# One lasting PSUM piece for the cell, scores ahead of updates, and another order on VectorE

## The chip, the cores and the metric

The kernel runs on one core of one Trainium2 chip. The metric is the device time of one execution in microseconds, given as the median of several runs. TensorE is called PE in the profile, VectorE DVE, ScalarE ACT, GpSimd POOL, and SyncE, which issues nearly all of the transfers, SP.

## The reference

An mLSTM cell over 4 batches, 8 heads, 768 time steps and head size 40, followed by a multiplicative feed-forward layer over the 3072 tokens with 320 features:

```python
for t in range(S):
    m_new = np.maximum(f_gate[:, :, t] + m, i_gate[:, :, t])
    f_stab = np.exp(f_gate[:, :, t] + m - m_new)
    i_stab = np.exp(i_gate[:, :, t] - m_new)
    C = f_stab[:, :, None, None] * C + i_stab[:, :, None, None] * np.einsum('bhd,bhe->bhde', vt, kt)
    n = f_stab[:, :, None] * n + i_stab[:, :, None] * kt
    h_tilde = np.einsum('bhde,bhe->bhd', C, qt)
    denom = np.maximum(np.abs(np.einsum('bhd,bhd->bh', n, qt)[:, :, None]), 1.0)
    y[:, :, t] = 1.0 / (1.0 + np.exp(-o_gate[:, :, t])) * h_tilde / denom
# x: y as (3072 tokens, 320)
out = ((x @ w1) * (x @ w2) @ w3) @ w_out      # d_ff = 1024
```

The four weights come as 64-bit floats and are turned into 32-bit floats on the chip.

## The kernel before, in words

**Chunks and units.** Time is cut into chunks of 64 steps. Two chunks (128 steps) of one batch, with all 8 heads, are a unit n; there are 24 units, and n runs over the 4 batches first. Inside a chunk the recurrence is a masked product: scores of k and q, times weights, times v; what the chunk inherits is the state times q.

**One step of the loop.** The main loop (L595) has 30 steps s. In a step it issues the loads two units ahead (`load`, `load_o`; `load_u` three ahead), the decay of the first state of the unit on POOL (`decayed`, L305), the turns of k and q (`turn`, L283: for n < 10 TensorE transposes `pt` and ScalarE copies, later a VectorE transpose), turns of y (`x_trans`, tile `px`), products of the feed-forward layer (`up`: tiles `pa` and `pb`; `ffn_out`: tile `po`; `w3_mm`: tile `wp`), and then the cell in `quarter_work` (L310). The ups are cut so that a small remainder (`rest`, 64-row matmuls) runs at the start of `quarter_work`; each up ends in a ScalarE copy `a_sb` and a VectorE product `ab`. From s = 4 on there is one up in a step, from s = 6 on there are two. Behind the cell VectorE converts pieces of the weights (`convert`), two or three in most steps up to s = 15.

**The cell.** `quarter_work(s)` issues the outputs of unit s-1 and the updates and scores of unit s, as small matmuls of 64 columns in quarters of the array. Its results lie in a tile `cell` of four PSUM banks, the only one of its pool (`bufs=1`):

```python
ss, pc, pi = part(0, 0, L), part(0, NP * L, D1), part(2, 0, D1)
ph = [t[halves[x], 2 + x, NP * D1:(NP + H) * D1].rearrange("p (h d) -> p h d", d=D1) for x in range(2)]
```

Banks 0 and 1 hold the scores `ss` and the updates `pc` of unit s; banks 2 and 3 hold what unit s-1 inherits (`pi`) and its own part (`ph`). The tile is taken anew in every step, so its first matmul waits until all readers of the tile of the step before are done. Within a step, accesses of different engines to the same bank wait for each other, and accesses to different banks do not.

**Order on TensorE before:** `ph`, `pi`, `pc`, `ss`. **Order on VectorE before:** the weights times scores (L348, tile `pw`), the second state (L352 or L354), the outputs (L369 and twice L373, tile `h`), the denominators (three small instructions from L378 on, tile `den`), the output gate (L383, tile `o_in`), y (L385), and last the third state (L362). The third state is the second one decayed by POOL (L307) plus the second half of `pc`.

**What sets the order.** TensorE's instructions are chained in the order written (`in_order`). For the first 17 steps all other engines keep the written order too (`keep_order`, `pinned = 17`), SP's and POOL's transfers among them; later a planner places instructions, except where `issue_after` ties them behind another one: the work behind the first read of `ss`, and the turns and conversions behind what `quarter_work` returns. Four more PSUM banks (`ps_m`) go round among all other matmul results while the cell runs.

## Time and profile before

| What | us |
|---|---|
| median of 11 runs | 472.02 |
| fastest and slowest of them | 469.83 and 474.42 |
| the profiled execution | 470.55 |
| its span on the core | 468.5 |
| TensorE busy in it | 446.8 |
| VectorE busy | 258.0 |
| ScalarE busy | 134.1 |
| POOL busy | 82.0 |

The span is what the profile covers of the execution; the rest of its time lies around it. A row of the profile gives line, engine, operation and tiles, as output<-inputs; nearly all matmuls carry line 90 or 93, those of the helpers, so they are told apart by their tiles. "PEld" is the load of weights into the array, which overlaps the matmuls. The busy time of TensorE holds pipelined instructions whose ends are modelled, so it tells that TensorE had work, not how well it was used. The row PEclk is the clock that TensorE was granted, in tenths of full speed, in 40 slices of 11.7 us.

### The profile page before, as it was taken

The numbers are of one execution on the slowest core, as the hardware profiler recorded it, in microseconds if no ns is written. First come the engines' busy times: TensorE is split into PE (matmuls) and PEld (weight loads), VectorE is DVE, ScalarE is ACT, GpSimd is POOL, SyncE is SP. The second block draws the span as 40 slices with busy tenths as digits, with TensorE's granted clock in tenths as the row PEclk, the third lists the DMA queues.
The fourth block names the chain that finished last, engine by engine and source line by source line (L and its number), as shares of the span: only waits on it lengthen the run. The fifth ranks groups of instructions, "written<-read, shape, count | busy, mean of one in ns | idle before, by whom it ended". The sixth has DMA issues, their size and how long they took to land.

```text
span 468.5 us, 12799 instructions
## 1 busy us (share of the span) xinstructions
PE 446.8 (95%) x5319; PEld 359.4 (77%) x5319; DVE 258.0 (55%) x515; ACT 134.1 (29%) x376; POOL 82.0 (17%) x156
## 2 busy tenths in 40 slices
PE   2867999999999999999999999999999999999997
PEld 2766788888778788887878777787777877868864
DVE  6675589888988988988832451615426133011110
ACT  3653274434533244223451220311101101011111
POOL 5341222222220221122161111200000000000000
PEclk9986699999999999999999999999999999999999
DMA  9999957688987676687462635444121120200001
GB/s 186 170 175 204 192 89 156 152 182 168 213 197 182 143 161 161 160 162 143 96 119 63 127 87 125 95 106 109 32 63 31 34 63 2 62 15 14 1 14 44
DMA packets 136554, 52.72 MB, mean 113 GB/s; under 512 B 109936, under 2 KB 127536, under 8 KB 136496
## 3 DMA queue, kind: packets, MB, share of 16 engines
q1 hardware_dynamic: 132896, 47.87, 49.8%
q10 hardware_dynamic: 3600, 4.03, 2.5%
q8 instruction: 42, 0.69, 0.7%
q14 instruction: 16, 0.13, 0.1%
HBM read 46.07 MB, written 5.80 MB: 111 GB/s over the span
## 4 chain that ended last, share of the span: by engine, by line
PE 93%; issue 2%; ACT 1%; DVE 1%; DMA 1%; POOL 1%; SPq 0%; DVEq 0%; POOLq 0%; ACTq 0%
PE pa L90 27%; PE po L90 22%; PE pb L90 18%; PE cell L90 13%; PE wp L90 7%; PE pt L93 2%; PE px L93 1%; DMA kbuf<-in_k_dram 1%; PE ub L90 1%; ACT pw L278 1%; POOL vw L302 0%; POOL pw L280 0%; SPq L444 0%; ACT qT L297 0%; PE pg L93 0%
## 5 line engine op out<-in xcount | busy, mean ns | idle before, releaser
L569 DVE TENSOR_TENSOR ab<-pb,a_sb 128x512 f32<-128x512 f32 x48 | 32.7, 689 | 140.7 <-ACT a_sb L568 140.7
L90 PE MATMUL po<-w3o,ab 128*128 128x320 f32 x384 | 106.2, 435 | 0.0
L90 PEld LDWEIGHTS po<-w3o,ab 128*128 128x128 f32 x384 | 72.1, 190 | 30.1 <-ACT a_sb L568 0.4
L90 PE MATMUL pa<-xT,w 128*128 128x256 f32 x384 | 92.8, 385 | 0.6 <-ACT xT L423 0.6
L90 PE MATMUL pb<-xT,w 128*128 128x256 f32 x384 | 91.7, 382 | 0.0
L90 PEld LDWEIGHTS pa<-xT,w 128*128 128x128 f32 x384 | 73.4, 193 | 13.5 <-ACT xT L423 1.0
L90 PEld LDWEIGHTS pb<-xT,w 128*128 128x128 f32 x384 | 73.8, 192 | 10.3
L568 ACT ACTIVATE a_sb<-pa 128x512 f32<-128x512 f32 x48 | 28.7, 597 | 170.2 <-PE pb L90 170.2
L307 POOL TENSOR_TENSOR state<-state,decay 128x164 f32<-128x164 f32 x40 | 21.9, 549 | 202.6 <-DVE state L352 113.6
L90 PE MATMUL pa<-xT,wr 64*64 64x256 f32 x384 | 47.0, 383 | 0.0
L90 PE MATMUL pb<-xT,wr 64*64 64x256 f32 x384 | 47.0, 383 | 0.0
L278 ACT ACTIVATE pw<-pw,aT 128x64 f32<-128x64 f32 x160 | 40.3, 337 | 14.8 <-DMA pw<-U_d 14.8
L90 PEld LDWEIGHTS pa<-xT,wr 64*64 64x64 f32 x384 | 25.8, 132 | 16.8 <-issue 7.8
L90 PE MATMUL wp<-wo,w3T 128*128 128x320 f32 x128 | 35.9, 433 | 0.6 <-DVE ab L569 0.6
L280 POOL TENSOR_SCALAR_AFFINE_SELECT pw<-pw 64x512 f32<-64x512 f32 x48 | 32.9, 686 | 19.0 <-ACT pw L278 17.5
L90 PEld LDWEIGHTS cell<-vbuf,pw 64*64 64x64 f32 x768 | 28.2, 144 | 9.3 <-issue 6.4
L90 PE MATMUL cell<-vbuf,pw 64*64 64x41 f32 x768 | 28.2, 234 | 5.6 <-issue 5.6
L348 DVE TENSOR_TENSOR pw<-cell,pw 128x512 f32<-128x512 f32 x24 | 16.6, 690 | 30.3 <-PE cell L90 30.3
L576 ACT COPY o_sb<-po 128x320 f32<-128x320 f32 x24 | 10.1, 420 | 75.5 <-PE po L90 71.6
L90 PEld LDWEIGHTS wp<-wo,w3T 128*128 128x128 f32 x128 | 23.7, 190 | 9.7 <-DVE ab L569 0.9
L90 PEld LDWEIGHTS pb<-xT,wr 64*64 64x64 f32 x384 | 25.8, 132 | 0.0
L373 DVE TENSOR_TENSOR h<-cell,h 64x328 f32<-64x328 f32 x48 | 23.9, 497 | 1.1
(90 smaller groups left out, 456.8 us busy)
## 6 DMA issues: line engine op xcount, KB each, us to landing
raw<-in_moe_w_dram SPq DMA_DIRECT2D x64, 128.0 KB, 3.1
pw<-U_d SPq DMA_DIRECT2D x40, 128.0 KB, 3.9
kbuf<-in_k_dram SPq DMA_DIRECT2D x24, 160.0 KB, 4.6
vbuf<-in_v_dram SPq DMA_DIRECT2D x24, 160.0 KB, 4.8
o_in<-in_o_gate_dram SPq DMA_DIRECT2D x24, 160.0 KB, 4.6
out_dram<-o_sb ACTq DMA_DIRECT2D x24, 160.0 KB, 2.0
raw<-in_moe_w_dram SPq DMA_DIRECT2D x7, 512.0 KB, 5.7
raw<-in_moe_w_out_dram SPq DMA_DIRECT2D x32, 80.0 KB, 2.4
```

The costliest lines, as they stand in the source:

```text
L90: in_order(nc.tensor.matmul(out, lhsT=lhsT, rhs=rhs, start=start, stop=stop))
L93: in_order(nc.tensor.transpose(out, in_, ident[0:n, 0:n]))
L278: nc.scalar.activation(out=pw[:, h, :], in_=src[:, h, :], func=AF.Exp, bias=aT[:, c, b * H + h:b * H + h + 1])
L280: nc.gpsimd.affine_select(out=pw[r], in_=pw[r], compare_op=OP.is_ge, fill=0.0, base=0, pattern=[[0, H], [1, L]], channel_multiplier=-1)
L307: nc.gpsimd.tensor_tensor(out=new, in0=old, op=OP.mult, in1=decay[:, b * NP:(b + 1) * NP, 2 * c + x:2 * c + x + 1] .to_broadcast([P, NP, D1]))
L348: first_read = nc.vector.tensor_tensor(out=pv, in0=ss, in1=pv, op=OP.mult)
L373: nc.vector.tensor_tensor(out=h[r], in0=ph[x], in1=h[r], op=OP.add)
L568: nc.scalar.mul(out=a_sb, in_=pa, mul=UP ** -2)
L569: nc.vector.tensor_tensor(out=ab_t[gr][j][:, fs[0]:fs[-1] + 1, t0:t0 + a_sb.shape[-1]], in0=pb, in1=a_sb, op=OP.mult)
L576: nc.scalar.copy(out=o_sb, in_=po)
```

## The change

Three things are changed in the cell, and nothing in the loads, the feed-forward layer or the order of the steps.

- The four banks are taken once, ahead of the loop, and serve all steps. There is no hand-over of the tile between steps any more; accesses to the same banks still wait for each other.
- On TensorE the scores `ss` are issued ahead of the updates `pc`.
- On VectorE the outputs (`h`) come first, then the weights (`pw`), the second state, the denominators, the third state, and last the output gate and y. For this `outputs` is cut into three: the part that reads PSUM, `first` (denominators) and `then` (gate and y). What `quarter_work` returns, behind which the turns and conversions are tied, is y in every step that has one.

```diff
@@ -72,6 +72,8 @@
     ps_c = cell_psum.enter_context(tc.tile_pool(name="ps_c", bufs=1, space=bass.MemoryType.PSUM))
     banks = [ps_m]
 
+    cell = ps_c.tile([P, 4, 512], FP, name="cell", tag="cell")
+
     def mps(shape, name):
         pool = banks.pop(0)
         banks.append(pool)
@@ -311,7 +313,7 @@
 
 
         rest()
-        t = ps_c.tile([P, 4, 512], FP, name="cell", tag="cell")
+        t = cell
 
         def part(j, c0, n):
             return t[:, j:j + 2, c0:c0 + NP * n].rearrange("p x (n d) -> p x n d", d=n)
@@ -336,17 +338,22 @@
             first, second, after = state[b]
             before_t[n] = first, second
             state[b] = after, second, first
+            kT, qT, pw = kT_t.pop(n), qT_t[n], u_t[n]
+            for p in range(NP):
+                for hip, x in quarters:
+                    mm(ss[halves[x], hip, p, :], kT[heads[hip], p, halves[x]], qT[heads[hip], p, halves[x]])
             for p in range(NP):
                 for x, e in quarters:
                     if x in ends:
                         mm(pc[halves[e], x, p, :], kt[halves[x], 2 * p + e, :], vw[halves[x], 2 * p + e, :])
-            kT, qT, pw = kT_t.pop(n), qT_t[n], u_t[n]
-            for p in range(NP):
-                for hip, x in quarters:
-                    mm(ss[halves[x], hip, p, :], kT[heads[hip], p, halves[x]], qT[heads[hip], p, halves[x]])
+        den = None
+        if 0 <= s - 1 < NU:
+            den = outputs(s - 1, pi, ph)
+        if n < NU:
             pv = pw.rearrange("p (n two) t -> p two n t", two=2)
             first_read = nc.vector.tensor_tensor(out=pv, in0=ss, in1=pv, op=OP.mult)
-            with tc.issue_after(first_read.ins):
+        with tc.issue_after(first_read.ins) if first_read else nullcontext():
+            if n < NU:
 
                 if c:
                     nc.vector.tensor_tensor(out=second, in0=pc[:, 0], in1=second, op=OP.add)
@@ -354,13 +361,13 @@
                     nc.vector.tensor_copy(out=second, in_=pc[:, 0])
                 if len(ends) > 1:
                     decayed(after, second, n, 1)
-        done = None
-        with tc.issue_after(first_read.ins) if first_read else nullcontext():
-            if 0 <= s - 1 < NU:
-                done = outputs(s - 1, pi, ph)
+            if den:
+                done = den()
             if n < NU and len(ends) > 1:
-                done = nc.vector.tensor_tensor(out=after, in0=pc[:, 1], in1=after, op=OP.add)
-        return done
+                nc.vector.tensor_tensor(out=after, in0=pc[:, 1], in1=after, op=OP.add)
+            if den:
+                done = done()
+        return done if den else first_read
 
     def outputs(n, pi, ph):
         c, b = divmod(n, B)
@@ -375,15 +382,23 @@
 
 
         den = sb.tile([P, H, 1], FP, name="den", tag="den")
-        nc.vector.tensor_scalar(out=den.bitcast(U32), in0=h[:, :, D:D1].bitcast(U32), scalar1=0x7FFFFFFF, scalar2=None,
-                                op0=OP.bitwise_and)
-        nc.vector.tensor_scalar(out=den, in0=den, scalar1=1.0, scalar2=2.0, op0=OP.max, op1=OP.mult)
-        nc.vector.reciprocal(out=den, in_=den)
-        e = o_t.pop(n)
-        nc.vector.scalar_tensor_tensor(out=e, in0=e, scalar=1.0, in1=den.to_broadcast([P, H, D]), op0=OP.add, op1=OP.mult)
-        y_t[n] = sb.tile([P, DM + REM], FP, name="y", tag="y")
-        return nc.vector.tensor_tensor(out=y_t[n][:, 0:DM].rearrange("p (h d) -> p h d", d=D), in0=h[:, :, 0:D], in1=e,
-                                op=OP.mult)
+
+        def first():
+            V = nc.vector
+            V.tensor_scalar(out=den.bitcast(U32), in0=h[:, :, D:D1].bitcast(U32), scalar1=0x7FFFFFFF, scalar2=None,
+                            op0=OP.bitwise_and)
+            V.tensor_scalar(out=den, in0=den, scalar1=1.0, scalar2=2.0, op0=OP.max, op1=OP.mult)
+            V.reciprocal(out=den, in_=den)
+            return then
+
+        def then():
+            e = o_t.pop(n)
+            nc.vector.scalar_tensor_tensor(out=e, in0=e, scalar=1.0, in1=den.to_broadcast([P, H, D]), op0=OP.add, op1=OP.mult)
+            y_t[n] = sb.tile([P, DM + REM], FP, name="y", tag="y")
+            return nc.vector.tensor_tensor(out=y_t[n][:, 0:DM].rearrange("p (h d) -> p h d", d=D), in0=h[:, :, 0:D],
+                                           in1=e, op=OP.mult)
+
+        return first
 
     def send(n):
 
```

## The prediction

> **What bounds the kernel now.** I read the page first (busy rows, clock row, chain), then the chain in order of time, the timeline where the chain shows gaps, and the transfers.

> ```profile
> span 468.5 us, 12799 instructions
> PE 446.8 (95%) x5319; PEld 359.4 (77%) x5319; DVE 258.0 (55%) x515; ACT 134.1 (29%) x376; POOL 82.0 (17%) x156
> ...
> PEclk9986699999999999999999999999999999999999
> DMA  9999957688987676687462635444121120200001
> ```

> TensorE is 95% busy and at full clock except between about 32 and 56 us (slices of 11.7 us), and the DMA engines are full (9) in the first five slices, to 58.6 us. The time is therefore the TensorE work plus what the start loses. The chain in order of time shows the loss:

> ```profile
> 29.55 3.13 issue
> 32.68 4.61 PE cell L90 x128
> 37.29 1.80 PE pt L93 x8
> 39.43 2.46 issue
> 41.90 3.82 PE cell L90 x105
> ...
> 165.79 2.32 PE cell L90 x123
> ```

> Columns are start, length, what. pt are the turns of k and q, px that of y, pa and pb the ups. The same cell block takes 4.61 us at 32.68 and 2.32 at 165.79. Two gaps of 3.13 and 2.46 us stand in front of cell blocks, put down to "issue", that is, to nothing the profile can name. From 70 us to the last matmul the chain has no gap over 0.7 us. The timeline names the gaps' end:

> ```profile
> 32.25 0.33 DVE L362 TENSOR_TENSOR state<-cell,state 128x164 f32<-128x164 f32 x1
> ...
> 32.65 1.71 PEld L90 LDWEIGHTS cell<-vbuf,pw 64*64 64x64 f32 x30 [3.36 <-issue]
> ...
> 41.47 0.33 DVE L362 TENSOR_TENSOR state<-cell,state 128x164 f32<-128x164 f32 x1
> ...
> 41.87 1.46 PEld L90 LDWEIGHTS cell<-vbuf,pw 64*64 64x64 f32 x31 [2.69 <-issue]
> ```

> Both times TensorE starts 0.07 us after the last VectorE read of the previous cell tile (32.58 to 32.65, 41.80 to 41.87). So the wait is the handing back of the whole four-bank tile, whose last reader is the third state update behind the y chain. In later steps the ups (6.9 us) and the remainders stand in between, and this wait is covered.

> **The change, part by part.** I number steps by s; ph, pi are the outputs' two matmul groups, pc the updates, ss the scores.

> *One lasting piece.* The release is gone; what stays are the waits between accesses of the same banks. ph and pi (banks 2, 3) now wait only for the three h reads and for the weights of the step before; ss and pc (banks 0, 1) for the third state read. At s=2: updates of step 1 end at 27.4 before. With scores first they end about 27.0 (copies of kT, qT end 25.58; 0.7 each for ss and pc). ub takes 1.1, so 28.1; the turns need q of step 2, issued at 24.02, landing 4.6 later, 28.6; they end about 29.2. ph and pi follow at once (1.5, at 30.7) instead of at 32.65. ss needs qT, whose copy ends at 32.03: ScalarE does the tanh of o_in first, and o_in lands at 26.66 + 3.9 = 30.56 whatever TensorE does. ss and pc run 32.1 to 33.3 (VectorE's third state read of step 1 is long done, POOL's vw ended 32.81 and can be 0.4 earlier). So cell 2 ends at 33.3 and not at 37.29: minus 4.0.

> *What is late next: the loads.* SP issues without a break from 19.9 to 59.2 us, the DMA engines are full, so the loads keep their times.

> ```profile
> 30.06 0.53 SPq L126 DMA_DIRECT2D q_all<-in_q_dram  x1
> ...
> 37.17 0.54 SPq L126 DMA_DIRECT2D kbuf<-in_k_dram  x1
> ```

> These are q for s=3 and k for s=4; the transfers' view gives 5.5 us to landing for the one (35.6) and 5.0 for the other (42.2). Turns of s=3 start about 34.9 with k (estimate, q's 5.5 used) and end between 36.2 (full clock) and 37.1 (half). px and the cell follow without the 2.46 gap: end at 39.0 at full clock (px 0.5, cell 2.3), 42.5 at half (0.8, 4.6); before 47.26. Either way s=4 waits for k until 42.2, so here the clock matters little. Turns end at 43.9 to 44.4 (q about 43.3); pa began 1.2 us behind the turns' end before (49.16 to 50.36, the copies of qT and xT on ScalarE), so 45.1 to 45.6 against 50.36: minus 4.8 to 5.3. From pa to the end of cell 4 it took 10.1 us, mostly at half clock; at full clock it is 3.46 + 0.5 + 0.9 + 2.4 = 7.3. So cell 4 ends at 52.4 to 55.7 against 60.5: minus 4.8 to 8.1.

> [...] In windows of 1 us (the clock is the third column from the end, behind the engines' busy times) the clock falls to 0.5 at about 32.04, rises at 38.87, falls at 42.28, rises at 55.92: the distances are 2, 1 and 4 times 3.41 us.

> ```profile
> 31.00:32.00 1.00, 0.00 (x0) 0.00 (x0) 0.96 (x2) 1.00 (x3) 0.85 (x3) 1.00 1.08 257
> 32.00:33.00 1.00, 0.32 (x7) 0.35 (x8) 0.97 (x3) 0.46 (x2) 1.00 (x2) 0.52 1.46 163
> ```

> [...] By the trace a gap of 2.46 us (39.43 to 41.90) lost the clock, and gaps of about 0.6 us (45.72, 49.79) kept it from coming back. The change still leaves a gap of up to 1.6 us at 33.3 and one of up to 3.2 at 39.0. [...]

> *Outputs first on VectorE.* The h reads can start when pi ends, 1.1 us before the cell's end, beside ss and pc. In a late step: the two ab end at 167.2, h three times (0.49 + 1.01) to 168.7, weights 0.69, state 0.32, denominators 0.8, third state 0.33, e and y 1.3: y at 172.2, against 172.9 before. Weights and second state come about 0.5 us later, so POOL's decay starts later, and behind it the masks (1.37), vw and the next decay: the next cell reads them some 10 us later. y being 0.7 earlier takes away TensorE's wait of 0.45 at 65.41 (px behind y): minus 0.4. The release of o_in for SP's next load hangs on y and comes earlier too. No DMA issue is moved.

> *A new wait.* The third state update now follows the second by only the denominators; it needs POOL's decay (0.47 plus two handoffs of about 0.1). The denominators take 0.8 to 0.9: covered. Bounds: nothing (a wait cannot gain), or 0.3 us on VectorE per step when POOL is still in the previous decay (0.70). e, y, the transposes and conversions, then the next ab queue behind it. Beyond 120 us VectorE has slack; between 61 and 120 (89 to 94% busy in the later slices) five steps make at most 1.5 us, against 1 us a step that VectorE gains by not waiting for the cell's end. I take zero.

> *Order of ss and pc on TensorE.* Same 128 matmuls. No row shows the price of ss after pi; bounds from the cell's own spread in the chain, 2.25 to 2.37 us: from minus 0.1 to plus 0.1 a step, about 2 us over 24 steps either way. I take zero.

> *Sum.* Minus 5.2 (4.8 + 0.4) to minus 8.5 (8.1 + 0.4). The loads cap it: k and q of s=6 land at 59.9 and about 60.5, where the turns began at 69.29, and behind the scaling of the next w_out piece (issued from 59.34) the copies of s=6 wait on ScalarE. I take minus 6.5. From there on everything hangs on TensorE's or VectorE's own pace and shifts as a whole; the weight loads of SP wait for VectorE's conversions and shift with them. The profiled execution took 470.55 (span 468.5 plus 2.05), so 464.05; it lies 1.5 under the median of the runs, which gives 465.5 for the median.

> **The rivals.** *The gain is half given back* (the freed time turns into waits for loads and a half clock that lasts to 56 us, or VectorE's conversions between 60 and 80 us hold ab): minus 2 to 4, 468 to 470. For it: the DMA share is above 1 in 19 of the 30 windows of 1 us from 30 to 60. Against: SP waits 4 us for VectorE at 59 to 69 us, so the loads there would move up. *Nothing changes*, because the gaps are something else (instruction fetch beside the full DMA engines; 0.63 at 45.72 has no releaser) or the dependence still spans the whole piece: minus 0.5, 471.5. Against: twice the same 0.07 us. *Slower: the cell itself stretches*, because VectorE now reads banks 2 and 3 while TensorE writes 0 and 1, in every one of 24 steps. It decides from 0.27 us a cell (6.5 / 24); at 0.5 (ss and pc, 1.1 us, half as fast again) the sum is plus 12 minus 6.5, 477.5. Against: ph took 1.02 us with no VectorE read beside it (57.99) and 1.02 with an ab read of PSUM beside it (165.61).

> **How the numbers follow.** Main case 0.68 (463.5 to 467), half given back 0.16, no change 0.07, slower 0.09. A measurement here can tell about 0.3% (1.4 us). So faster 0.84, same 0.07, slower 0.09. The range goes from 462.5 (8.5 and one more for the order) to 470 (end of the second case).

> **What would show it.** Right: no gap in front of ph at s=2 and s=3; the wait at s=3 and s=4 named after kbuf or q_all; pa of s=4 at 45 to 46; the cell still 2.3 us beyond 70; px at s=5 without wait; the cell of s=23 some 6 us earlier. Wrong: pa still at 50; a cell above 2.5 us in late steps; VectorE's third state waiting on POOL for more than 0.3 us a step; ab late, with TensorE waiting for a bank between 60 and 120.

## The result, and the profile after

The changed kernel takes 465.78 us (median; 463.12 to 468.85 in 12 runs) beside 472.01 us before (465.66 to 474.55, 47 runs): a ratio of 0.991, 95% interval 0.9881 to 0.9939. The forecast was 465.5. The total is right; several steps that led to it are not. A few executions of before and of three experiments took over 1.5% more than the fastest of their kernel; medians and ranges in the text are of all executions, the ratios leave these out.

The page after, first the span, the busy times, TensorE's granted clock and the share of the DMA engines (40 slices, now 11.5 us each):

```profile
span 461.4 us, 12788 instructions
PE 440.7 (96%) x5319; PEld 353.1 (77%) x5319; DVE 262.6 (57%) x515; ACT 134.9 (29%) x376; POOL 82.5 (18%) x156
...
PEclk9997999999999999999999999999999999999999
DMA  9999999797978567676353543535021120200001
```

The same 5319 matmul records take 6.1 us less of TensorE's time (446.8 before), out of 7.1 us of span. Granted clock in windows of a fraction of a microsecond: half speed from 32.0 to 38.9 and 42.3 to 55.9 us before (20.5 us), from 35.9 to 42.7 after (6.8 us). So between these two traces most of the gain is work that is now done at full clock. The trace after is of the shortest of its 12 executions (463.12 us), and traces of other kernels divide a gain of the same size differently, as the experiments show.

The chain in order of time (start, length, what), the stretch that the prediction was about:

```profile
29.61 2.49 PE cell L92 x115
32.10 1.26 issue
33.36 0.37 PE cell L92 x8
...
37.31 4.55 PE cell L92 x124
...
44.65 1.99 PE pa L92 x8
...
49.73 2.35 PE cell L92 x115
```

Cell blocks of s=2 and s=3 begin 3.1 and 4.6 us earlier (32.68 and 41.90 before); `pa` of s=4 begins at 44.65 and not 50.36; the cell of s=4 ends at 52.08 and not 60.54. From there on the kernel is only shifted: the block that took 2.32 us at 165.79 now ends 6.9 us earlier (161.23 against 168.11). A new gap of 1.26 us without a releaser stands inside the cell of s=2.

The timeline of TensorE after, the waits in front of the two cells and in front of `px` at s=5:

```profile
29.61 1.07 PE L92 MATMUL cell<-vbuf,pw 64*64 64x41 f32 x30 [1.06 <-DVE state L367]
...
37.31 1.83 PE L92 MATMUL cell<-vbuf,pw 64*64 64x41 f32 x30 [1.19 <-DVE state L367]
...
57.09 0.41 PE L95 MATMUL px<-ident,y 128*128 128x128 f32 x2 [0.34 <-DVE y L398]
58.58 0.33 PE L95 MATMUL px<-ident,y 128*128 128x128 f32 x1 [1.07 <-POOL y L428]
```

The first product of `ph` writes banks 2 and 3, and still waits for the third state (L367), which reads bank 1. And for the first of the `h` reads, which needs only banks 2 and 3, the view of its line says what it waited for (us in all, times), and VectorE's timeline when it began at s=4:

```profile
L376 DVE TENSOR_TENSOR h<-cell,gT x24: 483/500/501, 26.1 to 387.7; 128x328 f32<-128x328 f32 x24
...
  PE cell L92: 19.8, 20
...
52.11 0.50 DVE L376 TENSOR_TENSOR h<-cell,gT 128x328 f32<-128x328 f32 x1 [1.01 <-PE cell L92]
```

It starts when the cell ends (52.11 against 52.08), not when `pi` ends 1.0 us before. So one lasting piece of four banks is still one thing to the waits between engines; that accesses to different banks of it do not wait for each other, as the description of the kernel before has it, does not hold. Why, then, did the time fall where the prediction said, with the dependence that it had declared gone?

What changed is where the same wait stands. In the traces before and after no matmul and no weight load carries more than one wait (in each of the two, 263 of the 5319 weight loads carry one; a product's wait stands there); what else is waited for stands in a wait instruction of its own ahead of it (68 on TensorE in each, with two waits in 18 of them before and in 12 after). In front of the cell of s=2:

```
            wait instruction                        first product of ph
before      transfer of vbuf, DVE third state       TensorE itself (from the release of the old piece)
after       transfer of vbuf                        DVE third state
```

In the trace before, that wait instruction is recorded from 28.82 to 32.62 us, and the one in front of the cell of s=3 from 36.99 to 41.84; after, the wait instructions there take 0.05 us. The page names the same thing in its way: 5.6 us of idle in front of `ph` "<-issue" before, 2.2 us "<-DVE state L367" after. The next section asks which of these counts.

### The profile page after: what moved, and what is told of

The parts are those of the page before. It is cut to its first block, busy times and chain, and to the rows that moved or that the text cites. A ratio compares the mean times of both kernels' runs of the same rounds, so it can differ in the third digit from the quotient of the medians.

```text
span 461.4 us, 12788 instructions
## 1 busy us (share of the span) xinstructions
PE 440.7 (96%) x5319; PEld 353.1 (77%) x5319; DVE 262.6 (57%) x515; ACT 134.9 (29%) x376; POOL 82.5 (18%) x156
## 4 chain that ended last, share of the span: by engine, by line
PE 91%; DVE 4%; issue 1%; DMA 1%; ACT 1%; POOL 1%; SPq 0%; DVEq 0%; POOLq 0%; ACTq 0%
PE pa L92 27%; PE po L92 23%; PE pb L92 18%; PE cell L92 12%; PE wp L92 8%; PE pt L95 1%; PE px L95 1%; DMA kbuf<-in_k_dram 1%; DVE pw L354 1%; DVE h L380 1%; DVE h L376 0%; PE ub L92 0%; DVE ma L191 0%; ACT kT L299 0%; POOL pw L282 0%
## 5 line engine op out<-in xcount | busy, mean ns | idle before, releaser
L92 PE MATMUL pa<-xT,w 128*128 128x256 f32 x384 | 91.0, 380 | 0.8 <-ACT xT L438 0.8
L92 PEld LDWEIGHTS pa<-xT,w 128*128 128x128 f32 x384 | 72.3, 190 | 13.2 <-ACT xT L438 1.0
L309 POOL TENSOR_TENSOR state<-state,decay 128x164 f32<-128x164 f32 x40 | 19.2, 481 | 207.0 <-DVE den L388 155.3
L92 PE MATMUL wp<-wo,w3T 128*128 128x320 f32 x128 | 35.9, 433 | 1.1 <-DVE ab L584 1.1
L282 POOL TENSOR_SCALAR_AFFINE_SELECT pw<-pw 64x512 f32<-64x512 f32 x48 | 34.3, 715 | 13.1 <-ACT pw L280 11.5
L92 PEld LDWEIGHTS cell<-vbuf,pw 64*64 64x64 f32 x768 | 26.8, 138 | 6.0 <-DVE state L367 2.8
L92 PE MATMUL cell<-vbuf,pw 64*64 64x41 f32 x768 | 26.8, 228 | 2.2 <-DVE state L367 2.2
L304 POOL TENSOR_TENSOR vw<-vbuf,wT 128x328 f32<-128x328 f32 x24 | 19.6, 818 | 22.3 <-PE cell L92 20.8
```

The source lines that it names most:

```text
L92: in_order(nc.tensor.matmul(out, lhsT=lhsT, rhs=rhs, start=start, stop=stop))
L282: nc.gpsimd.affine_select(out=pw[r], in_=pw[r], compare_op=OP.is_ge, fill=0.0, base=0, pattern=[[0, H], [1, L]], channel_multiplier=-1)
L304: nc.gpsimd.tensor_tensor(out=vw_t[n], in0=vbuf[n % NB], op=OP.mult, in1=wT[:, c, b * H:(b + 1) * H].unsqueeze(2).to_broadcast([P, H, D1]))
L309: nc.gpsimd.tensor_tensor(out=new, in0=old, op=OP.mult, in1=decay[:, b * NP:(b + 1) * NP, 2 * c + x:2 * c + x + 1] .to_broadcast([P, NP, D1]))
```

## The experiments

Each of the three parts alone, and a kernel in which the waits really are bank by bank, beside before at 470.82 us (466.23 to 475.85, 23 runs).

**The lasting piece alone** (e1_lasting_only), before with

```diff
+    cell = ps_c.tile([P, 4, 512], FP, name="cell", tag="cell")
-        t = ps_c.tile([P, 4, 512], FP, name="cell", tag="cell")
+        t = cell
```

> Before, with the four banks taken once and nothing else changed. The piece theory (the gain is the missing hand-over: ph waits only for readers of its own two banks): the gaps ahead of the cells of s=2 and s=3 go, and most of the 6 us are here, 466 to 468. The order theory (the whole piece is still waited for, and the gain comes from what stands last among its readers): ph of s=2 and s=3 still starts 0.07 us behind the third state, gaps of about 3.1 and 2.5 us stay, time within 1 us of before.

Measured: 466.30 us (465.31 to 467.82, 6 runs), ratio 0.9904 [0.9876, 0.9933]. The lasting piece alone brings a gain as large as the whole change's. Its timeline:

```profile
32.65 1.82 PE L92 MATMUL cell<-vbuf,pw 64*64 64x41 f32 x30 [3.10 <-DVE state L364]
...
41.75 1.07 PE L92 MATMUL cell<-vbuf,pw 64*64 64x41 f32 x30 [2.17 <-DVE state L364]
...
48.02 1.99 PE L92 MATMUL pa<-xT,w 128*128 128x256 f32 x8 [0.84 <-ACT xT L425]
```

The two cells start at nearly the same times as before (32.68, 41.90), after nearly the same waits (3.15 and 2.48): the wait of which the prediction expected everything is still there in full. But the cell of s=3 has no gap inside (0.63 us at 45.72 before), the clock comes back at 46.15 instead of 55.92, and `pa` starts 2.3 us earlier.

**Scores ahead of updates alone** (e2_scores_only) and **VectorE's new order alone**, with a fresh piece and the updates first (e3_order_only):

```diff
 # e2: before, with the block of ss moved ahead of the block of pc
-            [pc] [ss]
+            [ss] [pc]
 # e3: after, with
-        t = cell
+        t = ps_c.tile([P, 4, 512], FP, name="cell", tag="cell")
 #     and the block of pc ahead of ss again
```

> Before, with the scores issued ahead of the updates and nothing else. Piece theory: minus 0.5 at most. Order theory: the cell of s=0 ends about 1.0 us earlier (the scores no longer wait behind vw), the cell of s=1 about 1.4 us earlier (26.0 against 27.4); the gap ahead of the cell of s=2 stays at about 3 us; in all minus 1 to minus 2.

> Before, with VectorE's new order alone (outputs, weights, second state, denominators, third state, gate, y), the piece taken anew in each step and updates first. Piece theory: no gain beyond 0.5 us. Order theory: the third state ends 1.4 to 1.6 us earlier behind the cell's end, the gaps shrink from 3.1 and 2.5 to about 1.5 and 1 us, minus 3 to minus 5.

Measured: 470.85 us, ratio 0.9988 [0.995, 1.0026], and 470.40 us, ratio 0.9989 [0.9955, 1.0023]. Neither differs from before by anything that can be told. Both traces have gaps inside a cell without a releaser: 2.36 and 2.85 us in the scores-only kernel (at 35.70 and 47.06), 1.51 us in the other.

**Two lasting pieces of two banks** (e4_two_pieces), the changed kernel with

```diff
-    cell = ps_c.tile([P, 4, 512], FP, name="cell", tag="cell")
+    cell = [ps_c.tile([P, 2, 512], FP, name=f"cell{i}", tag=f"cell{i}") for i in range(2)]
-            return t[:, j:j + 2, c0:c0 + NP * n]...
+            return cell[j // 2][:, :, c0:c0 + NP * n]...
```

and `ph` in the second one.

> The changed kernel, with the four banks as two lasting pieces of two banks (scores and updates; inherited part and own part). Piece theory: the same as the changed kernel, since bank by bank is what it already waits for. Order theory: now h starts when pi ends, about 1.0 us ahead of the cell's end, and ph of s=2 and s=3 waits for the weights and h and not for the third state: gaps under 0.5 us at s=2, the loads are the next wait; minus 0 to minus 3 us against the changed kernel, 463 to 466.

Measured: 464.65 us (463.84 to 465.40, 6 runs), ratio 0.9866 [0.984, 0.9892]. Here the waits are what the prediction had assumed for one piece. VectorE's timeline at the cell of s=4, whose last products run until 54.41 us:

```profile
53.56 0.50 DVE L375 TENSOR_TENSOR h<-cell,gT 128x328 f32<-128x328 f32 x1
```

`h` starts at the end of `pi` (53.47), 0.8 us before the cell is done. It is the lowest median of all kernels run, some 1.1 us under the changed one; the two ratios' intervals overlap. The clock has a smaller part in it:

```profile
32.00:49.00 17.00, 15.22 (x191) 12.67 (x192) 15.16 (x31) 6.45 (x17) 6.15 (x11) 0.50 1.05 205
```

From 32 to 49 us it stands at 0.50 (third column from the end), nearly as long as the 20.5 us before, and TensorE's busy time is 444.2 us: 2.6 us less than before, out of 6.5 us of span (462.0). Here most of the gain is idle time that is gone.

The next four ran beside before at 471.28 us (467.45 to 474.77, 28 runs).

**The changed kernel with a fresh piece** (e5_after_fresh), after with only the lasting piece undone:

> The changed kernel, with the four-bank piece taken anew in each step as before; both orders as changed. Piece theory: the gaps of about 3 and 2.5 us are back, 470 to 472. Order theory: the same as the changed kernel within 1 us, ph of s=2 starting at about 29.6 and of s=3 at about 37.3, each 0.07 us behind the third state.

Measured: 469.53 us (468.17 to 471.90, 12 runs), ratio 0.9981 [0.9951, 1.0011]. The gain is gone: both new orders together bring nothing measurable without the lasting piece. Its trace has the third state's wait short (the cell of s=2 begins at 31.46) and gaps of 2.40 us and 0.66 us inside the cells of s=2 and s=3.

**Two lasting pieces and both old orders** (e6_two_pieces_old_order):

> Before, with two lasting pieces of two banks and both old orders (updates first, weights first on VectorE). No reordering, but no wait for the third state either: ph waits for h alone. Both theories give a gain here if the clock theory holds: gaps at s=2 and s=3 under 0.7 us, the clock at half for less than 10 us (about 17 before), minus 4 to minus 7. If the order on VectorE matters by itself, less than half of that.

Measured: 465.19 us (464.61 to 466.55, 6 runs), ratio 0.9884 [0.9843, 0.9926]. Nothing is lost without the new orders.

**Before, with TensorE kept busy in the two waits** (e7_before_warm): products of the identity, whose results are unused, ahead of the cells of s=2 and s=3.

```diff
         rest()
+        if s in FILL:                      # FILL = {2: 13, 3: 11}
+            warm = mps([P, 512], "warm")
+            for _ in range(FILL[s]):
+                mm(warm[:, 0:128], ident, ident)
```

> Before, with products of the identity (13 at s=2, 11 at s=3, results unused) on TensorE in front of the cell, about where it waits. Nothing that the change does is in it: the wait for the third state stays. Clock theory (most of the gain is the clock that the gaps cost): the clock stays full up to at least 42 us, the cells of s=2 and s=3 take about 2.4 us in place of 4.6, minus 3 to minus 6. If the gaps themselves are the loss: same as before or up to 2 us slower.

Measured: 466.70 us (465.76 to 468.51, 11 runs), ratio 0.9916 [0.9887, 0.9944]. The row of its granted clock:

```profile
PEclk9759999999999999999999999999999999999999
```

From 34.5 us on the clock is full. The cell of s=2 starts at 36.21, 3.5 us later than before, and `pa` of s=4 still starts 2.2 us earlier (48.12). Two things differ from before: the clock in these steps, and the place of the code, which the products shift by 24 matmuls; the gap inside a cell (1.58 us) moves from s=3 to 63.90 us. How the gain divides between the two this run doesn't say.

**Before, with the third state ahead of the output gate and y** (e8_third_state_early): `outputs` returns gate and y as a function that is called behind the third state.

> Before, with the third state ahead of gate and y on VectorE and nothing else (weights, second state, outputs, denominators, third state, gate, y; fresh piece, updates first). Order theory: like the whole new order on VectorE, since only the place of the last reader counts: the third state ends about 1.3 us earlier behind the cell; minus 3 to minus 5. If it is the outputs' place that counts: under 1 us.

Measured: 468.53 us (465.74 to 469.78, 12 runs), ratio 0.9936 [0.9908, 0.9965]. The waits in front of the cells of s=2 and s=3 fall to 1.54 and 1.01 us; gaps of 1.61 and 0.63 us stand inside them (the trace is of the shortest execution). This kernel gains some 2.7 us with a fresh piece; that the shorter wait brings them is not shown, since VectorE's new order alone and the changed kernel with a fresh piece have the third state early too (waits of 1.13 and 1.41 us in front of the cell of s=3) and gain nothing that can be told.

```profile
q8 instruction: 1, 0.02, 10.9%
```

With the lasting piece alone, the one packet between 26 and 37 us lies from 30 to 31:

```profile
q8 instruction: 1, 0.02, 8.3%
```

The table puts the two packets beside the start of the cell that waits for the third state, s=2 and s=3 (us):

| kernel | third state's wait stands | cell of s=2, packet | cell of s=3, packet | gap inside s=2, s=3 |
|---|---|---|---|---|
| before | wait instruction | 32.7, 33.7 | 41.9, 43.4 | none, 0.63 |
| scores only | wait instruction | 33.3, 35.4 | 43.0, 47.6 | 2.36, 2.85 |
| VectorE's order only | wait instruction | 31.3, 33.7 | 41.0, 42.0 | 1.51, none |
| after, fresh piece | wait instruction | 31.5, 33.9 | 41.0, 42.8 | 2.40, 0.66 |
| third state early | wait instruction | 31.1, 33.3 | 40.5, 42.2 | 1.61, 0.63 |
| lasting piece only | first product | 32.7, 30.8 | 41.8, 37.9 | none, none |
| after | first product | 29.6, 30.4 | 37.3, 37.4 | 1.26, none |

Where the wait stands in an instruction of its own, the packet comes 1.0 to 4.6 us after the cell has begun; where the first product carries it, 0.8 us after at the latest and up to 3.8 before. In the two kernels with two pieces, whose cells do not wait for the third state, it comes at 30.6 and 37.7 us and at 30.7 and 38.3, as in the others with a lasting piece. Where the idle time was filled, the added products stand ahead of the wait instruction, and the packets come ahead of the cells (33.0 and 40.1 us, cells at 36.2 and 43.4). Every gap ends 2.3 to 3.2 us after its packet (before: 43.4 to 46.35; after: 30.4 to 33.36; the pages' DMA row shows 9 at both). The theory to be tested goes no further than this table: the place of the wait decides when the packet comes, and with it whether the gain is there. What in the chip would tie the packet to the wait, no trace shows. Four kernels test it by moving the place of the wait; by it the gain is gone in the first and there in the other three. The first three ran beside before at 472.22 us (466.03 to 474.89, 25 runs).

**Lasting piece, the wait pushed back into a wait instruction** (e9_lasting_wait_in_sequencer), and **the same product without that wait** (e10_lasting_product_no_wait):

```diff
 # e1, ahead of the cell
+        if s in (2, 3):
+            hold = mps([P, 512], "hold")
+            mm(hold[0:L, 0:1], ident[0:D, 0:L], state[s - 1][0][heads[0], 0, 0:1])   # e9: the third state
+            mm(hold[0:L, 0:1], ident[0:D, 0:L], ident[0:D, 0:1])                     # e10, in place of it
```

> Before plus the lasting piece, and ahead of the cells of s=2 and s=3 one one-column product that reads the third state of the step before and writes a feed-forward bank. In the compiled program the wait for VectorE's third state then stands in a separate wait instruction on TensorE, as it does in before (where it is pushed there by the wait on TensorE itself that the fresh tile brings), and not on the first matmul of ph. [...] Rival (the lasting piece gains by dropping the hand-over itself, wherever the wait stands): 466.3, packets at 30.8 and 38.0.

> The same as the run with the wait, but the product reads the identity, so it waits for nothing of the cell, and the first matmul of ph carries the wait for the third state itself. Theory: as the lasting piece alone, 466.3 us, packets at about 30.8 and 38.0, no gap in the middle of the cell of s=3. Rival (the two extra products or the shift of the code by one matmul are what counts): the same as the run with the wait, 470 or more.

Measured: 473.26 us (466.60 to 475.97, 12 runs), ratio 1.0017 [0.9967, 1.0067], with the wait; 465.90 us (463.24 to 468.54, 8 runs), ratio 0.9893 [0.985, 0.9936], without. Two one-column products that differ in the operand they read take the whole gain away, or leave it. Without the four longest executions of the first its median is 472.35 us, 6.4 us above the second's. The timeline of the first:

```profile
33.15 0.23 PE L92 MATMUL hold<-state,ident 40*64 40x1 f32 x1 [2.32 <-DVE state L367]
38.18 0.69 PE L92 MATMUL cell<-qT,kT 40*64 40x64 f32 x10 [0.53 <-issue]
43.49 0.23 PE L92 MATMUL hold<-state,ident 40*64 40x1 f32 x1 [2.08 <-DVE state L367]
50.39 0.92 PE L92 MATMUL cell<-qT,kT 40*64 40x64 f32 x25 [2.84 <-issue]
```

and of the second:

```profile
32.67 1.82 PE L92 MATMUL cell<-vbuf,pw 64*64 64x41 f32 x30 [2.85 <-DVE state L367]
41.77 1.15 PE L92 MATMUL cell<-vbuf,pw 64*64 64x41 f32 x30 [2.02 <-DVE state L367]
```

TensorE waits about as long for the same third state in both. In the first the packets come at 35.4 and 47.3 us, 2.2 and 3.8 us after the wait, and the gaps (0.53 and 2.84 us) end 2.8 and 3.1 us after them; in the second they come at 31.5 and 39.8, within the waits, and there is no gap inside the two cells. The clock differs too: at half for 30.7 us in the first (28.55 to 59.27), for 17.1 us in the second. (The first trace is of an execution of 474.1 us, one of the long ones; the second of 468.5, the longest of its kernel.)

**Fresh piece, the wait on a product** (e11_fresh_wait_on_product) and **lasting piece, the wait on the same product** (e12_lasting_wait_on_product; beside before at 471.26 us, 11 runs): a one-column product into an unused column of the piece of the step before, which waits for that piece's last reader.

```diff
+        if s in (2, 3):
+            mm(old[0][0:L, 0, 500:501], ident[0:L, 0:L], ident[0:L, 0:1])   # e11; in e12 cell[0:L, 0, 500:501]
         t = ps_c.tile([P, 4, 512], FP, name="cell", tag="cell")             # e12: t = cell
```

> Before, with the piece taken anew in each step, both old orders, and ahead of the cells of s=2 and s=3 one one-column product into an unused column of the piece of the step before. That product carries the wait for the third state on itself; the wait instruction behind it then waits for a transfer only, and the first matmul of ph for TensorE itself. Theory: the code is fetched while the product waits (packets at about 31 and 38 us), no gap in the middle of the cell of s=3, 466 to 467 us without any lasting piece. Rival (the hand-over of the fresh piece costs in itself): 470 to 471.5, as before. [...]

> Before plus the lasting piece, with the same one-column products ahead of the cells of s=2 and s=3 as in the run with the fresh piece and the wait on the product; here no matmul of the cell then waits for TensorE itself. It differs from that run, whose median stayed at 472.4 us, in the piece alone. If the products cost there (one more matmul that the cell stands behind, or the shift of the code by one matmul), it stays at 470 to 472.5 here too. If the fresh piece costs in itself, beyond the place of the wait (the wait of the first matmul on TensorE itself, which leaves TensorE idle for about 0.3 us, or something that the one profile of that run did not show), it is 466 to 467 here. [...]

Measured: 472.39 us (467.36 to 475.36, 12 runs), ratio 1.0004 [0.996, 1.0048], with the fresh piece; 466.59 us (465.58 to 468.99, 6 runs), ratio 0.9894 [0.9853, 0.9935], with the lasting one. The second is as the theory has it: packets at 31.1 and 37.8, no gap inside the two cells. The first is not. Its trace does show the packets early (30.7 and 36.2) and no gap:

```profile
32.22 0.27 PE L91 MATMUL cell<-ident 64*64 64x1 f32 x2 [0.99 <-DVE state L366]
40.31 0.27 PE L91 MATMUL cell<-ident 64*64 64x1 f32 x2 [2.19 <-DVE state L366]
```

but this is of its shortest execution, 467.4 us, and the median is 5 us longer. In its program a wait instruction (for the transfer of `vbuf`) stands behind the waiting product, and the first product of `ph` waits for TensorE itself; in the other neither is there. Whether one of these makes the other executions longer, or the fresh piece costs something else, one trace does not tell. This stays open, and with it whether the place of the wait is all that the lasting piece changes.

## Why the prediction was right in the total, and where its steps failed

**The lasting piece frees `ph` from the third state: failed.** The waits hold for the whole four-bank piece; `ph` waits for the third state as before (L367 in the timeline, 3.10 and 2.17 us with the lasting piece alone). The sentence "ph and pi (banks 2, 3) now wait only for the three h reads and for the weights of the step before" is true of two pieces, not of one. What the lasting piece did take away is the wait for TensorE itself, and with it the reason for the third state's wait to stand in an instruction of its own. With the lasting piece kept, putting it back there cost the whole gain (a ratio of 1.0017 against 0.9893, some 6 us). The prediction had both halves of this among its rivals ("the dependence still spans the whole piece", "instruction fetch beside the full DMA engines"), and gave them 0.07 as reasons for no change. The first was right. The second named what the traces show beside the gaps: instruction packets 2.3 to 3.2 us ahead of each gap's end.

**Minus 5.2 to minus 8.5, taken as minus 6.5: the size held, with other terms.** The gaps in front of the cells shrank (3.15 and 2.48 to 1.06 and 1.19 us) because the steps before them ended earlier and the third state came before gate and y, not because the wait was gone; 1.26 us came back inside the cell of s=2. So that the sum met 465.78 so closely was in part luck: a term that stayed was taken as gone, and the place of the wait, for which the sum had no term, brought the time instead (1.0017 against 0.9893). The prediction had the cell of s=2 end at 33.3 (33.7), `pa` of s=4 at 45.1 to 45.6 (44.65), the cell of s=4 end at 52.4 to 55.7 (52.08). That the loads would cap it was right in part: in front of the turns of s=3 TensorE waits 0.55 us for `kbuf` and 0.26 for `q_all`, in front of those of s=4 for nothing.

**The half clock: a part of it stayed.** Minus 6.5, between the two ends of the sum, was the author's estimate. 6.8 us are left of 20.5: the clock is at half from 35.9 to 42.7, behind gaps of 1.26, 0.55 and 0.26 us, and from `pa` of s=4 to the end of its cell, at full clock, it took 7.4 us (44.65 to 52.08), where the prediction had 7.3 for that. Which of the gaps, if any, brought the clock down, no run tells. Between the two traces the clock is also the largest term, 6.1 of 7.1 us. That it is so for the medians is not shown. The mean granted clock of each execution is on record: its median is 0.985 after and 0.971 to 0.974 before, but the changed kernel with a fresh piece has 0.982 and no gain that can be told, the lasting piece with the wait on the product 0.976 and a gain of 4.7 us, and 7 of 87 executions of before have 1.0 and took 470.19 to 473.67 us, no less than the others. Of these 7 no trace was kept.

**`h` at the end of `pi`, y 0.7 us earlier, `px` of s=5 without wait: failed.** `h` starts at the cell's end. y ended 4.72 us after the cell of s=4 before (65.26 and 60.54), and 4.87 us after it now (56.95 and 52.08). `px` waits 1.41 us where it waited 0.45. The last product needs POOL's copy of the tail of y, and POOL is late. First its copy in the timeline before, then the timeline after:

```profile
65.40 0.24 POOL L413 COPY y<-y 128x64 f32<-128x64 f32 x1 [0.48 <-DVE y L385]
...
55.10 1.51 POOL L282 TENSOR_SCALAR_AFFINE_SELECT pw<-pw 64x512 f32<-64x512 f32 x2
56.70 0.84 POOL L304 TENSOR_TENSOR vw<-vbuf,wT 128x328 f32<-128x328 f32 x1
57.51 0.64 POOL L309 TENSOR_TENSOR state<-state,decay 128x164 f32<-128x164 f32 x1
58.09 0.43 POOL L428 COPY y<-y 128x64 f32<-128x64 f32 x1
```

Before, POOL had been idle for 0.48 us when y came. The prediction had seen that the decay and the masks come later, and asked only who reads the masks; it did not follow that queue to the copy of y.

**Costs taken as zero: right.** The third state waited for POOL once, 0.6 us in all, as it did before. Late cells take 2.29 to 2.35 us (2.25 to 2.37 before), so the order of `ss` and `pc` costs nothing that can be seen there; the rival of the stretched cell is out, though its condition was not met, since `h` starts at the cell's end. Both orders by themselves measured 0.9988 and 0.9989.

**Still open:** the median with the fresh piece and the wait on the product; and how a late packet goes with 5 or 6 us. Before has one gap of 0.63 us inside a cell; the kernel with the scores ahead has gaps of 2.36 and 2.85 us and takes no longer, and no run changed the gaps without the clock.

## What to carry to other kernels

Look at where a wait stands, not only at whom it waits for: here, with the wait for the third state in an instruction of its own, the instruction packet came 1.0 to 4.6 us after the start of the cell, and with the same wait on the first matmul 0.8 us after it at the latest; with the lasting piece kept, putting the wait back into an instruction of its own gave a ratio of 1.0017 in place of 0.9893. The tile handed out anew added just the one wait (for its own engine) that stood on the matmul in place of this one, so where a tile returns to the same place each time, take it once; and if engines are to work on different banks at a time, give the banks different tiles (`h` began 0.8 us ahead of the cell's end with two, at its end with one). When a gap has no releaser, look for the instruction packets before calling it noise, and look at the clock behind it as well as at its length.

## What was not expected of the hardware

- Gaps of 0.5 to 2.9 us inside a cell ended 2.3 to 3.2 us after an instruction packet of 16 KB, and in the kernels with the wait in an instruction of its own, except where added products stood in front of it, that packet came 1.0 to 4.6 us after the wait's end.
- Behind gaps of 1.3 us and less TensorE stood at half clock for 6.8 us (35.90 to 42.73, after), and a single one of 0.63 us stands at the start of a stretch in which before stayed at half clock for 9.8 us longer than the kernel without it (55.92 against 46.15).
- The changes of the clock lie 6.83, 3.41 and 13.65 us apart in the trace before (32.04, 38.86, 42.28, 55.93) and 6.83 us apart in the trace after (35.90, 42.73). Before spread over 9 us (465.7 to 474.6 in 47 runs), the kernels with lasting pieces over 1.6 to 5.7 us (in 6 to 12), all but the one with the wait put back (9.4 us); no run shows what makes this spread.
